# Sliding-window attention in pairs of tiles, with 64-column score pieces and one shared block of small triangles

## The chip, the cores and the metric

The kernel runs on one core of a Trainium2 chip. A core has TensorE (matmuls, here PE; its weight loads are PEld), VectorE (DVE), ScalarE (ACT), GpSimd (POOL) and SyncE (SP), which only issues transfers. Each engine works off its own list of instructions in order; semaphores tie the lists together. The metric is the device time of one execution in microseconds (us), lower is better.

## What is computed

One transformer block on x of 2048 rows and 448 columns, in bf16. The conditioning vector gives six rows (shift, scale and gate of each half). With h a layer norm of x, scaled and shifted:

```
q, k, v = h @ wqkv                      # 16 heads of 28
scores  = q k^T / sqrt(28), kept where 0 <= i - j < 256, else -1e9
x = x + ga * (softmax(scores) @ v) @ wo
h = layernorm(x) * (1 + cb) + sb
z = gelu(h @ w_in)                      # 1792 columns: z1 and z2, 896 each
g = w_sp @ layernorm(z2) + b_sp         # w_sp is 2048 x 2048
x = x + gb * (z1 * g) @ w_out
```

## The kernel before

The rows are 16 tiles of 128. All work is cut into operations, each with a name, an engine (or a choice of engines), what it needs and which buffers it holds. A stored list, `ORDER`, gives the order of all operations: a number is an operation by its order of creation, `/n` picks its buffer and `.n` its engine. `Planner.emit` (L115) turns this into one list for each engine, with waits. So nothing is planned at run time: each engine goes through its list and stops where a wait isn't met.

**Projections.** `project` (L775 on) multiplies the transposed, modulated rows hT by the weights. The 448 rows of contraction lie in four chunks of 128, of which chunks 1 and 2 overlap; one half of one of them holds zeros or is left out. A chain of four full matmuls gives one group of four heads of Q or K for a block of rows (blocks of 1, 1, 2, 4, 4 and 4 tiles), or V of one tile. ScalarE or VectorE evicts the result into QKT or Vaug (L806, L809, L818, L821). In the second half of the block, z2 (`z2m`) and z1 (`z1m`) come from hT and w_in in the same chunks; there the class `Pair` (L734) makes two chains of three full matmuls and one operation `_r` with both half chunks, 64 rows each, which run beside each other in two row strips of the array.

**Attention** (L862 to L960), tile by tile. For tile j the keys of tiles j-2, j and j-1 matter. For each of these a visit of 16 matmuls (`s_mm`, 28 rows by 128 columns, heads in four row strips of the array) puts scores of all 16 heads into four banks. Two exponentials (L908, 128 x 1024 elements each, two banks) write them to a slot of PT. For the tiles j-2 and j the window cuts a triangle, and GpSimd zeroes it with an affine select over 512 32-bit pairs (L914). Eight matmuls (`pv_fn`, columns of 32 beside each other) multiply each slot by V, with the sum of the exponentials in a column of ones. So a whole tile has three visits, six exponentials and four selects; in all there are 90 exponentials and 60 selects.

VectorE transposes the result (`oq`, L940), takes the reciprocal, VectorE or GpSimd normalises (`nrm`, L945), VectorE transposes again (`oT`, L949), four matmuls multiply by wo, and VectorE adds to x (`x1`, L959). Layer norm, a transposing transfer and a modulation give the second hT.

**The second half.** GELU on ScalarE (L1018, L1014 for z2, L1037 for z1), the layer norm of z2 on VectorE, then 28 products of 16 full matmuls each with the transposed w_sp (`G`), whose parts lie where QKT, Vaug and PT lay, so that their transfers wait for the end of attention. VectorE adds and multiplies (L1106, L1108); `out` matmuls, a last addition (L1128) and the stores end the kernel.

**Shapes on TensorE.** Score visits run in four row strips, products with V in four column strips, half chunks in two row strips, the rest on the whole array. `column_tiles` (L104) lets whole matmuls that stand next to products with V run as four column strips. All matmuls go through `mm` (L451 to L457), so they share these lines in the profile and are told apart by tiles and shapes.

## Time and profile before

| | us |
|---|---|
| time, median of 3 runs | 269.65 (269.1 to 269.99) |
| span of the profiled execution, first to last instruction | 267.2 |
| between the span and the median | 2.45 |
| DVE / ACT / POOL busy in the span | 166.0 / 133.2 / 103.8 |

The profile gives no separate time for its own execution; its span stands beside the runs' median. Its rows name an engine, a line, an operation and the tiles, with the count; then busy time in total, the mean of one in ns, and the engine's idle time just before with what ended it. Sums by stage give, for a stretch of the span, the busy time and the count of each engine. The chain is followed back from the last instruction through what released each step.

### The profile page before, as it was taken

The page shows a single profiled execution, that of the slowest core. Times are in us where ns is not written, and L with a number is a line of the kernel's source. Part 1 is how long each engine was busy: PE and PEld are TensorE (multiplying, and loading weights), DVE is VectorE, ACT ScalarE, POOL GpSimd, SP SyncE. Part 2 cuts the span into 40 slices and gives each one's busy share as a digit, 9 for nine tenths or more (in the row PEclk, how much of TensorE's full clock was granted, in tenths as well). Part 3 has the DMA queues.
Part 4 walks back from the last instruction along what each step waited for, and adds up shares of the span by engine and source line. Part 5 has one row for each costly group of instructions (what it writes and reads, how often), then busy time and mean ns, then how long its engine had stood idle before and what let it go on. Part 6 is the DMA issues. An engine that isn't in the chain of part 4 may idle for free.

```text
span 267.2 us, 7093 instructions
## 1 busy us (share of the span) xinstructions
PE 258.8 (97%) x3059; PEld 127.8 (48%) x3059; DVE 166.0 (62%) x389; ACT 133.2 (50%) x182; POOL 103.8 (39%) x163
## 2 busy tenths in 40 slices
PE   6799999999999899999999999999999999999996
PEld 2676455554554444544444444444444444444553
DVE  4789987878789999488888730722033071327553
ACT  4899899999999999977687100000000000000100
POOL 3774799997989866436532300000000000000000
PEclk9999999999999999999999999999999999999999
DMA  6974260371998341789799950000000000000133
GB/s 225 352 194 56 42 178 5 71 122 23 172 212 195 65 100 39 124 118 164 157 191 215 165 97 0 2 0 0 0 0 2 0 0 0 2 0 17 52 101 108
DMA packets 61020, 23.83 MB, mean 89 GB/s; under 512 B 49854, under 2 KB 60861, under 8 KB 60989
## 3 DMA queue, kind: packets, MB, share of 16 engines
q1 hardware_dynamic: 60715, 22.92, 41.0%
q8 instruction: 24, 0.39, 0.7%
q10 hardware_dynamic: 274, 0.46, 0.5%
q14 instruction: 7, 0.06, 0.1%
HBM read 9.47 MB, written 1.84 MB: 42 GB/s over the span
## 4 chain that ended last, share of the span: by engine, by line
PE 76%; ACT 14%; DMA 3%; DVE 3%; SPq 1%; POOL 1%; issue 1%
PE ps L457 71%; ACT PT L908 12%; PE ps L454 5%; DMA wqk_raw<-in_A_wqkv_dram 2%; DMA hT<-xn 2%; ACT QKT L806 1%; DVE w_out_sb L964 1%; POOL PT L914 1%; ACT hT L683 1%; SPq L488 1%; DVE oq L940 1%; DVE oT L949 0%; PE ps L772 0%; POOL xn L620 0%; SPq L505 0%
## 5 line engine op out<-in xcount | busy, mean ns | idle before, releaser
L908 ACT ACTIVATE PT<-ps 128x1024 bf16<-128x1024 f32 x90 | 84.5, 1059 | 2.3 <-PE ps L457 1.7
L1037 ACT ACTIVATE z1T<-ps 128x512 bf16<-128x512 f32 x28 | 15.1, 599 | 100.9 <-PE ps L457 100.8
L1106 DVE TENSOR_TENSOR tmpg<-ps,bsp_bc 128x512 bf16<-128x512 f32 x28 | 18.8, 688 | 60.9 <-PE ps L457 60.6
L457 PE MATMUL ps<-QKT,z 128*128 128x512 bf16 x224 | 50.0, 379 | 0.0
L914 POOL TENSOR_SCALAR_AFFINE_SELECT PT<-PT 128x512 f32<-128x512 f32 x60 | 36.8, 635 | 5.1 <-ACT PT L908 5.1
L457 PEld LDWEIGHTS ps<-QKT,z 128*128 128x128 bf16 x224 | 21.9, 98 | 26.4 <-ACT z2raw L1018 0.2
L607 POOL TENSOR_TENSOR rs_all<-ve_all,neghalf 128x1 f32<-128x1 f32 (+2 forms) x27 | 18.6, 692 | 27.8 <-DVE ve_all L606 26.7
L457 PE MATMUL ps<-w_spC,z 128*128 128x512 bf16 x112 | 25.8, 379 | 0.0
L457 PE MATMUL ps<-w_spD,z 128*128 128x512 bf16 x112 | 25.8, 379 | 0.0
L457 PE MATMUL ps<-hT,w_in_sb 128*128 128x512 bf16 (+1 forms) x101 | 25.2, 380 | 0.0
L457 PE MATMUL ps<-w_in_sb,hT 128*128 128x448 bf16 (+1 forms) x110 | 24.4, 353 | 0.4 <-DVE oq L940 0.2
L620 POOL TENSOR_SCALAR xn<-x_sb,rs_all,nm_all 128x512 bf16<-128x512 bf16 x26 | 20.2, 782 | 4.7 <-DVE nm_all L611 3.0
L457 PE MATMUL ps<-w_out_sb,z1T 128*128 128x448 bf16 (+2 forms) x119 | 21.9, 341 | 0.0
L457 PE MATMUL ps<-hT,WQK 128*128 128x512 bf16 (+2 forms) x123 | 21.1, 307 | 0.7 <-ACT QKT L806 0.7
L599 DVE BATCH_NORM_STATS2 st_all<-x_sb 128x6 f32<-128x448 bf16 x32 | 19.3, 615 | 3.0 <-DMA x_sb<-in_A_x_dram 2.8
L599 DVE BATCH_NORM_STATS2 st_all<-z2raw 128x6 f32<-128x448 bf16 x32 | 19.3, 618 | 2.1 <-ACT z2raw L1018 1.8
L457 PE MATMUL ps<-QKT 28*128 28x128 bf16 x720 | 18.3, 217 | 1.5 <-ACT PT L908 1.4
L457 PEld LDWEIGHTS ps<-QKT 28*128 28x128 bf16 x720 | 10.4, 92 | 15.6 <-ACT PT L908 11.3
L809 DVE CAST QKT<-ps 128x512 bf16<-128x512 f32 (+2 forms) x26 | 16.1, 624 | 2.8 <-PE ps L457 1.8
L457 PEld LDWEIGHTS ps<-w_spC,z 128*128 128x128 bf16 x112 | 10.9, 98 | 13.4 <-DVE ve_all L606 0.4
L457 PEld LDWEIGHTS ps<-w_spD,z 128*128 128x128 bf16 x112 | 11.0, 98 | 13.2
L457 PEld LDWEIGHTS ps<-w_out_sb,z1T 128*128 128x128 bf16 x119 | 11.6, 98 | 9.9
(93 smaller groups left out, 319.3 us busy)
## 6 DMA issues: line engine op xcount, KB each, us to landing
wmod_sb<-in_w_mod_dram SPq DMA_DIRECT2D x8, 224.0 KB, 4.3
w_in_sb<-in_B_w_in_dram SPq DMA_DIRECT2D x8, 224.0 KB, 4.3
out_dram<-fin SPq DMA_DIRECT2D x16, 112.0 KB, 1.7
x_sb<-in_A_x_dram SPq DMA_DIRECT2D x3, 448.0 KB, 6.6
bsp_bc<-in_B_b_sp_dram SPq DMA_DIRECT2D x1, 512.0 KB, 4.7
wqk_raw<-in_A_wqkv_dram SPq DMA_DIRECT2D x1, 452.0 KB, 5.6
wmod_sb<-in_w_mod_dram SPq DMA_DIRECT2D x1, 448.0 KB, 4.5
wmod_sb<-in_w_mod_dram ACTq DMA_DIRECT2D x1, 448.0 KB, 4.8
```

What stands on the lines that cost most here:

```text
L454: last = e.matmul(out_[32 * j:32 * j + 32], lhsT=lhsT[:, 32 * j:32 * j + 32], rhs=rhs, start=st, stop=sp, tile_position=(0, 32 * j), **kw)
L457: return e.matmul(out_, lhsT=lhsT, rhs=rhs, start=st, stop=sp, **kw)
L488: return load(name, prio, lambda e: e.dma_start(x_sb[:, t0:t0 + n, :], x_d[:, t0:t0 + n, :]), n * 128 * D * 2, order=order)
L599: st = [dve("%sst%d" % (name, i), prio, dve_ns(D), lambda e, i=i, s_=s_: e.bn_stats(st_all[:, slot, t, i, :], s_()), deps, tens) for i, s_ ...
L607: r = pool(name + "rs", prio, 420 + 148 * n, lambda e: e.tensor_tensor(rs_all[:, slot, t0:t1], ve_all[:, slot, t0:t1], neghalf[:, t0:t1], ...
L620: return e.tensor_scalar(dst, src, rs_all[:, slot, t:t + 1], nm_all[:, slot, t:t + 1], ALU.mult, ALU.add)
L683: last = e.activation(d, s_, ACT.Identity, bias=a, scale=k)
L809: return e.tensor_copy(QKT[:, g, cols], ps[:, ten.slot, 0:w])
L908: e_op = P.op("E%d_%d" % (j, ui), pr, [("act", 925, lambda e, e_in=e_in, e_out=e_out: e.activation(e_out(), e_in(), ACT.Exp, scale=SCALE)) ...
L914: ready = pool("M%d_%d" % (j, ui), pr - 50, pool_ns(512), lambda e, pt=pt, pat=pat, cm=cm, cmp=cmp: e.affine_select(out=pt32(pt.slot), in_ ...
L1037: g = P.op("z1g%d_%d" % (tb, ft), pr - 19, [("act", act_ns(512), lambda e: e.activation(z1T[:, ft, tb * 512:(tb + 1) * 512], ps[:, ten.slo ...
L1106: a = dve("ga%d_%d" % (tb, ft), pr, dve_ns(512), lambda e, tb=tb, ten=ten, tg=tg: e.tensor_tensor(tmpg[:, tg.slot, :], ps[:, ten.slot, :], ...
```

## The change

Tiles 0 and 1 stay as they were. From tile 2 on attention goes by pairs (j, j+1) in five visits, each with two exponentials:

- E, twice (two groups of heads each): keys of tiles j-2 and j-1, that is 64 columns of the first and 192 of the second for each head, eight 64-column pieces to a bank.
- C, once: the four small triangles of 64 by 64 for each head and tile (keys of the own tile's half, and of the tile two back), 64 matmuls of 28 rows by 64 columns and 64 moving columns, in four row strips and two column strips. Two selects split the block: `Mb` writes one kind of triangle to a buffer of its own, then `Ma` zeroes the other kind in place.
- L, twice: keys of tiles j and j+1, again 192 and 64 columns.

E and L each need one select over 256 pairs. In all there are 76 exponentials and 88 selects. A product with V (`PV..._p`, `_m`, `_d` for the tiles two back, one back and own) now takes its two 64-column halves from different slots, and needs both E or L visits of its heads. The slots lie in PT, and six more in rows of z2 and z1T that are free until attention ends; the z2 normalisations of tiles 5 to 8 and the GELUs of z1's last columns wait for all products with V.

`Pair` is replaced by `chunks`: one chain of three full matmuls and one half one, `_r`, free to stand anywhere. The projections of the blocks from the third on use it too, and there the order picks for each `_r` whether it runs whole or half. The warm-up matmuls go from 22 to 14. `ORDER` is a new list of 1735 operations. Among other things it gives ScalarE 2 more evictions of Q or K, 4 of V and 5 of z2, GpSimd 5 normalisations and 7 xn fewer and 5 modulations more, and in the first microseconds takes five operations off ScalarE's list ahead of its first exponential. Its numbers are left out here.

```diff
+    PTS = [z2_off + 9 * FH * 2 - 6144 + 2048 * i for i in range(3)] + [z1_end - 6144 + 2048 * i for i in range(3)] + [pt_off + 2048 * i for i in range(NPT)]
+    assert 6144 <= 4 * FH * 2 and z1_off + 8 * 6 * D <= z1_end - 6144
+
+    def ptv(slot, off, dims):
+        v = arena[:, PTS[slot] // 2 + off:PTS[slot] // 2 + off + 1]
+        return bass.AP(v.tensor, v.offset, [list(v.ap[0])] + dims)
+
+    def pt32(slot, off, dims):
+        v = arena[:, PTS[slot] // 2 + 2 * off:PTS[slot] // 2 + 2 * off + 2].bitcast(F32)
+        return bass.AP(v.tensor, v.offset, [list(v.ap[0])] + dims)
...
+    def chunks(name, prio, side, opts, deps, stat, mov, n, joint=None, idx=0, rprio=None, padded=False):
+
+        ten = joint if joint else Ten(opts, guard=True)
+        acc = Acc()
+
+        def out_ap():
+            return ps[:, joint.got[idx][1] if joint else ten.slot, 0:n]
+        ops = []
+        for c_ in (0, 3, 1 + side):
+            o = [None]
+
+            def fn(e, c_=c_, o=o):
+                return mm(e, out_ap(), stat(c_, slice(0, 128)), mov(c_, slice(0, 128)), acc.first is o[0], acc.last is o[0])
+            o[0] = pe("%s_%d" % (name, c_), prio, mm_ns(n), fn, deps(c_), [ten], order=ops[:1], accs=[acc])
+            ops.append(o[0])
+        c_, rows, pos = (2, slice(64, 128), (64, 0)) if side == 0 else (1, slice(0, 64), (0, 0))
+        r = [None]
+
+        def rest(e):
+            return mm(e, out_ap(), stat(c_, rows), mov(c_, rows), acc.first is r[0], acc.last is r[0], tile_position=pos)
+
+        def whole(e):
+            return mm(e, out_ap(), stat(c_, slice(0, 128)), mov(c_, slice(0, 128)), acc.first is r[0], acc.last is r[0])
+        r[0] = P.op(name + "_r", prio if rprio is None else rprio, [("pe", mm_ns(n), f) for f in ([whole] if padded else []) + [rest]],
+                    [deps(c_), padded or []], [ten], order=ops[:1], mode=(FREE, 64) if padded else 64, accs=[acc])
+        ops.append(r[0])
+        return ops, ten
...
+                elif b >= 2:
+                    ops, ten = chunks("qk%d_%d" % (b, g), p_, g // 4, B_D, lambda c_, u=u, g=g: [t_wqkp[u // 2][3][(g // 4, c_)], hT_op[b][c_]],
+                                      lambda c_, r, g=g: WQK[r, c_, 4 * g:4 * g + 4, :].rearrange("p a b -> p (a b)"), lambda c_, r: hT[r, c_, cols], w, padded=[z_wq[g // 4]])
+                    proj[b].extend(ops)
...
+    def exp_op(name, pr, s_op, tens, e_in, e_out, pt):
+        return P.op(name, pr, [("act", 925, lambda e: e.activation(e_out(), e_in(), ACT.Exp, scale=SCALE))], [s_op, t_exp0], tens + [pt], table="exp")
+
+    def keep(name, pr, n, slot_in, slot_out, off, dims, pattern, base, cm, cmp, deps, tens):
+        return pool(name, pr, pool_ns(n), lambda e: e.affine_select(
+            out=pt32(slot_out.slot, off, dims), in_=pt32(slot_in.slot, off, dims), pattern=pattern, compare_op=cmp, fill=0.0, base=base, channel_multiplier=cm), deps, tens)
+
+    def pv_op(name, pr, gp, kb, acc, pv_ten, tens, deps, mov):
+        o = [None]
+
+        def fn(e):
+            last = None
+            for s_ in range(2):
+                for g in range(4):
+                    last = mm(e, pvo(pv_ten.slot, g, 2 * gp + s_), Vaug[:, kb, 4 * g + 2 * gp + s_, :], mov(g, s_),
+                              s_ == 0 and acc.first is o[0], s_ == 1 and acc.last is o[0], tile_position=(0, 32 * g), skip_group_check=True)
+            return last
+        o[0] = pe(name, pr + G["pv"], 8 * 14, fn, [deps, V_op[kb]], tens + [pv_ten], accs=[acc], mode=33)
+        return o[0]
...
+    def tile_pair(j):
+        unit = {}
+
+        def visit(kind, gh, pr):
+            gs = (2 * gh, 2 * gh + 1) if kind != "C" else (0, 1, 2, 3)
+            tens = [Ten(B_S), Ten(B_S)]
+            k0 = {"E": j - 2, "L": j, "C": j}[kind]
+
+            def s_mm(e):
                 last = None
+                if kind == "C":
+                    for g in gs:
+                        for t in (j, j + 1):
+                            for h, kt in ((0, t), (1, t - 2)):
+                                for r in range(4):
+                                    c = 128 * g + 64 * (t - j)
+                                    last = mm(e, ps[64 * h:64 * h + 64, tens[r // 2].slot + r % 2, c:c + 64],
+                                              QKT[32 * r:32 * r + DH, 4 + g, kt * 128 + 64 * h:kt * 128 + 64 * h + 64],
+                                              QKT[32 * r:32 * r + DH, g, t * 128 + 64 * h:t * 128 + 64 * h + 64], True, True, tile_position=(32 * r, 64 * h))
+                    return last
+                for gl, g in enumerate(gs):
+                    for kt, q0, n, c in ((k0, j * 128, 1, 6), (k0 + 1, j * 128, 3, 0)) if kind == "E" else ((k0, j * 128 + 64, 3, 2), (k0 + 1, j * 128 + 192, 1, 0)):
+                        for r in range(4):
+                            v = ps[:, tens[r // 2].slot + r % 2, 64 * (c + gl):64 * (c + gl) + 1]
+                            last = mm(e, bass.AP(v.tensor, v.offset, [list(v.ap[0]), [128, n], [1, 64]]), QKT[32 * r:32 * r + DH, 4 + g, kt * 128:(kt + 1) * 128],
+                                      QKT[32 * r:32 * r + DH, g, q0:q0 + 64 * n], True, True, tile_position=(32 * r, 0))
+                return last
+            keys = {"E": (j - 2, j - 1), "L": (j, j + 1), "C": (j - 2, j - 1, j, j + 1)}[kind]
+            deps = [QK_op[(g, blk[j])] for g in gs] + [QK_op[(4 + g, blk[k])] for g in gs for k in keys]
+            nm = "%s%d_%d" % (kind, j, gh)
+            s_op = pe("S" + nm, pr - 50, 270, s_mm, deps, tens, mode=32)
+            pair_S.setdefault(j, []).append(s_op)
+            for gp in range(2):
+                pt = Ten(B_C if kind == "C" else B_EL)
+                nmu = "%s%d" % (nm, gp)
+                ready = exp_op("E" + nmu, pr, s_op, [tens[gp]], lambda ten=tens[gp]: ps[:, ten.slot:ten.slot + 2, :].rearrange("p b n -> p n b"),
+                               lambda pt=pt: ptv(pt.slot, 0, [[2, 512], [1, 2]]), pt)
+                if kind == "E":
+                    ready = keep("M" + nmu, pr, 256, pt, pt, 256, [[64, 4], [1, 64]], [[0, 4], [-1, 64]], 0, 1, ALU.is_gt, [ready], [pt])
+                elif kind == "L":
+                    ready = keep("M" + nmu, pr, 256, pt, pt, 0, [[64, 4], [1, 64]], [[0, 4], [1, 64]], 64, -1, ALU.is_ge, [ready], [pt])
                 else:
+                    ptb = Ten(B_B)
+                    dims = [[64, 8], [1, 64]]
+                    mb = keep("Mb" + nmu, pr, 512, pt, ptb, 0, dims, [[0, 8], [-1, 64]], -64, 1, ALU.is_gt, [ready], [pt, ptb])
+                    ma = keep("Ma" + nmu, pr, 512, pt, pt, 0, dims, [[0, 8], [1, 64]], 0, -1, ALU.is_ge, [ready, mb], [pt])
+                    unit[("B", gp)] = (ptb, mb)
+                    ready = ma
+                unit[(kind, gh, gp)] = (pt, ready)
+        for n_, (kind, gh) in enumerate((("E", 0), ("E", 1), ("C", 0), ("L", 0), ("L", 1))):
+            visit(kind, gh, j + 0.4 * n_)
+
+        def seg2(a, oa, b, ob):
+            return ptv(a.slot, oa, [[(PTS[b.slot] - PTS[a.slot]) // 2 + ob - oa, 2], [2, 64]])
+        for t in (j, j + 1):
+            odd = t - j
+            pv_ten, acc = Ten(B_PV), Acc()
+            pvs = []
+            for gp in range(2):
+                E, L = [unit[("E", gh, gp)] for gh in range(2)], [unit[("L", gh, gp)] for gh in range(2)]
+                C, B = unit[("C", 0, gp)], unit[("B", gp)]
+                A = L if odd else E
+                pvs.append(pv_op("PV%d_p%d" % (t, gp), t, gp, t - 2, acc, pv_ten, [E[0][0], E[1][0], B[0]], [E[0][1], E[1][1], B[1]],
+                                 lambda g, s_, E=E, B=B, odd=odd: seg2(E[g // 2][0], 128 * (6 - 2 * odd + g % 2) + s_, B[0], 256 * g + 128 * odd + s_)))
+                pvs.append(pv_op("PV%d_m%d" % (t, gp), t, gp, t - 1, acc, pv_ten, [A[0][0], A[1][0]], [A[0][1], A[1][1]],
+                                 lambda g, s_, A=A, odd=odd: ptv(A[g // 2][0].slot, 128 * (4 * odd + g % 2) + s_, [[256, 2], [2, 64]])))
+                pvs.append(pv_op("PV%d_d%d" % (t, gp), t, gp, t, acc, pv_ten, [C[0], L[0][0], L[1][0]], [C[1], L[0][1], L[1][1]],
+                                 lambda g, s_, C=C, L=L, odd=odd: seg2(C[0], 256 * g + 128 * odd + s_, L[g // 2][0], 128 * (2 - 2 * odd + g % 2) + s_)))
+            pv_of[t] = (pvs, pv_ten)
...
-            need = [rs] + (proj_all if t >= 9 else raw_users)
+            need = [rs] + (proj_all if t >= 9 else raw_users) + (all_PV if 5 <= t <= 8 else [])
...
-                    z1T[:, ft, tb * 512:(tb + 1) * 512], ps[:, ten.slot, :], ACT.Gelu_apprx_tanh))], deps + mod_done, [ten], table="gelu")
+                    z1T[:, ft, tb * 512:(tb + 1) * 512], ps[:, ten.slot, :], ACT.Gelu_apprx_tanh))], deps + mod_done + (all_PV if ft >= 5 else []), [ten], table="gelu")
...
-    for i in range(22):
+    for i in range(14):
```

310 lines of the change are left out of this document (135 added, 175 removed).

## The prediction

> **What bounds the kernel now.** I began with the page's first part and its chain, which name TensorE, and then asked how far to trust them: the sums by stage, the instructions in order of time, and the waits.
>
> ```profile
> span 267.2 us, 7093 instructions
> PE 258.8 (97%) x3059; PEld 127.8 (48%) x3059; DVE 166.0 (62%) x389; ACT 133.2 (50%) x182; POOL 103.8 (39%) x163
> ...
> PE 76%; ACT 14%; DMA 3%; DVE 3%; SPq 1%; POOL 1%; issue 1%
> ```
>
> TensorE is called busy for 97% of the span and carries 76% of the chain; ScalarE comes second with 14%. The sums by stage (PE, PEld, DVE, ACT, POOL from left to right) show where ScalarE's part lies:
>
> ```profile
> 0.00:10.00 10.00, 7.22 (x79) 3.87 (x82) 4.75 (x18) 5.71 (x12) 4.18 (x17) 1.00 0.83 263
> 10.00:20.00 10.00, 9.26 (x178) 6.69 (x164) 8.82 (x28) 9.63 (x27) 7.96 (x12) 1.00 0.88 252
> 20.00:30.00 10.00, 9.83 (x271) 5.82 (x270) 9.04 (x23) 9.16 (x15) 5.22 (x9) 1.00 0.28 40
> 30.00:70.00 40.00, 39.95 (x865) 20.88 (x867) 32.75 (x72) 39.10 (x44) 37.44 (x54) 1.00 0.41 92
> 70.00:120.00 50.00, 47.92 (x981) 24.03 (x972) 42.12 (x98) 47.11 (x55) 34.53 (x51) 1.00 0.67 121
> 120.00:264.60 144.60, 144.60 (x711) 66.50 (x709) 68.12 (x153) 22.46 (x34) 14.47 (x25) 1.00 0.29 57
> ...
> 75.00:92.00 17.00, 15.35 (x403) 8.25 (x392) 15.19 (x36) 17.00 (x20) 14.94 (x22) 1.00 0.82 168
> ```
>
> From 120 to 264.6 us TensorE has no gap at all and ScalarE is nearly idle. From 30 to 70 us ScalarE is busy for 39.10 of 40 us, but TensorE, given other work in the same order, for 39.95. Only between 75 and 92 us does a full ScalarE (17.00 of 17.00) leave TensorE 1.65 us short. So the exponentials are not the length of this kernel: they cost what TensorE loses waiting for them.
>
> A matmul's busy time runs past the start of the next, so "busy" can hide waiting. The starts in order of time tell more:
>
> ```profile
> 41.62 1.27 PE L457 MATMUL ps<-hT,WQK 128*128 128x512 bf16 x5
> 42.82 0.40 PE L457 MATMUL ps<-QKT 28*128 28x128 bf16 x16
> 43.16 1.69 PE L457 MATMUL ps<-hT,WQK 128*128 128x512 bf16 x7
> 44.77 0.40 PE L457 MATMUL ps<-QKT 28*128 28x128 bf16 x16
> 45.11 1.05 PE L454 MATMUL ps<-hT,WQK 128*32 128x512 bf16 x16
> 45.98 0.87 PE L457 MATMUL ps<-PT,Vaug 128*32 128x128 bf16 x48
> 46.78 0.40 PE L457 MATMUL ps<-QKT 28*128 28x128 bf16 x16
> ...
> 161.69 1.46 PE L457 MATMUL ps<-QKT,z 128*128 128x512 bf16 x6
> 162.98 1.03 PE L457 MATMUL ps<-w_spC,z 128*128 128x512 bf16 x4
> 163.84 2.32 PE L457 MATMUL ps<-QKT,z 128*128 128x512 bf16 x10
> ```
>
> In the late stage six 512-column matmuls take 162.98 - 161.69 = 1.29 us, 0.215 us each: 0.42 ns a column. A visit of 16 score matmuls, four beside each other in four row strips, streams 4 x 128 columns, 0.215 us, but 43.16 - 42.82 = 0.34 us pass until the next work starts. The seven full matmuls behind it need 7 x 0.215 = 1.51 us and take 1.61. So each change of TensorE's tile shape costs about 0.12 us (0.10 and 0.125). Sorting the old order by tile shape I count 119 changes, 115 of them from the first score visit on: some 14 us, the largest loss there is. What is truly waited for is small:
>
> ```profile
> PE ps L457 <- ACT PT L908: 1.4, 4, 0.4
> PE ps L457 <- DVE oq L940: 0.2, 1, 0.2
> PE ps L454 <- DVE hT L697: 0.2, 1, 0.2
> ...
> PEld ps L457 <- ACT PT L908: 11.7, 30, 0.6
> ...
> 83.51 0.40 PE L457 MATMUL ps<-QKT 28*128 28x128 bf16 x16 [0.43 <-ACT PT L908]
> ```
>
> (Both answers cover 20 to 120 us; the last row, in order of time, is the longest of the four waits.) The weight loads' 11.7 us are mostly the shape change and the running matmul; the stages above leave 0.17 + 0.05 + 2.08 = 2.3 us of open gap from 20 to 120 us. With what hides under running matmuls I call the recoverable waiting 2.3 to 5 us. The Trainium skill, in "Trainium Kernel Development and Optimization" under "Performance Expectations", says that matmul busy time is a bad measure because matmuls are pipelined; by it the 97% would hide more, and the starts above agree that busy is not the same as streaming.
>
> **The change, part by part.**
>
> Exponentials, 90 to 76, and what the new order moves onto ScalarE and off GpSimd:
>
> ```profile
> L908 ACT ACTIVATE PT<-ps 128x1024 bf16<-128x1024 f32 x90 | 84.5, 1059 | 2.3 <-PE ps L457 1.7
> L818 ACT ACTIVATE Vaug<-ps 128x448 bf16<-128x448 f32 x3 | 1.6, 545 | 0.0
> L914 POOL TENSOR_SCALAR_AFFINE_SELECT PT<-PT 128x512 f32<-128x512 f32 x60 | 36.8, 635 | 5.1 <-ACT PT L908 5.1
> L531 POOL TENSOR_SCALAR_AFFINE_SELECT ident<-ident 128x128 bf16<-128x128 bf16 x1 | 0.3, 292 | 0.1
> L945 POOL TENSOR_TENSOR o_sb<-oq,rec_all 128x448 bf16<-128x448 f32 x13 | 12.2, 942 | 8.5 <-DVE rec_all L941 8.4
> L620 POOL TENSOR_SCALAR xn<-x_sb,rs_all,nm_all 128x512 bf16<-128x512 bf16 x26 | 20.2, 782 | 4.7 <-DVE nm_all L611 3.0 <-DVE nm_all L637 1.7
> ```
>
> 14 x 84.5/90 = 13.1 us leave ScalarE; it takes over eleven evictions (2 of Q or K, 4 of V, 5 of z2, near 0.545 us each: 6 us) and gives two early ones to other engines: about 8 us lighter. GpSimd's selects go from 60 to 88, of which 56 have 256 columns. No row shows that form; it lies between the 128-column select (0.292) and the 512-column one (0.635), and on the line between them near 0.41: 56 x 0.41 + 32 x 0.635 = 43.3 us against 38.1, +5.2 (-0.4 to +17.8 with 0.31 to 0.635 each). GpSimd loses five normalisations (0.942), seven xn (0.782) and gains five modulations: it ends some 2 us lighter. Both engines get slack; neither decides. Of the waiting of 2.3 to 5 us I take **-2.0 us** (from +1 to -4.5, since the new order has waits of its own: each diagonal product now needs one shared block and two late blocks, so three exponentials and their selects, and all that stands behind it in TensorE's order waits too). Two waits are new beyond attention: the GELUs of z1's columns from 640 on and the z2 normalisations of tiles 5 to 8 now wait for every product with V, because their rows hold exponentials until then. Behind the first such GELU stand ScalarE's other GELUs, and TensorE's banks behind those; in the new order it comes after the last products are issued, so I cost it at nothing, with up to 1 us if the last product is late (inside the +1 above).
>
> Score matmuls. Before, a tile has three visits; now a pair has five. E and L visits keep 16 matmuls and 512 columns' worth of streaming, 0.215 us (in each row strip 64 then 192 columns, 0.225 with a little for the short ones). The shared visit issues 64 matmuls of 64 columns on strips of 28 rows by 64 columns, a form that no row shows. If all eight strips stream together it is 8 x 64 columns, 0.22 us. At the other end stand the shortest matmuls of the trace, on the whole array, one behind the other:
>
> ```profile
> 6.36 0.44 PE L457 MATMUL ps<-sc_sb,wmod_sb 128*128 128x1 bf16 x12
> 6.67 0.60 PE L457 MATMUL ps<-warm 128*128 128x256 bf16 x4
> ```
>
> 12 in 0.31 us: 0.026 us each, so 64 in a row would be 1.65 us. The nearer row is the score visit: its sixteen matmuls start in four groups and the next weights are loaded meanwhile. I take twice the best, 0.43 us. Streaming of all score visits: before 46 visits, 45 x 0.215 = 9.7 us; now 3 x 0.215 for the first two tiles (two half visits and two whole), 28 x 0.225 and 7 x 0.43: 10.0 us, **+0.3** (-1.2 to +8.9).
>
> "TensorE: Matmul & The Clock Gate" of the Trainium skill, under "Back-to-back issue gap", puts a matmul of up to 64 columns at about 60 cycles, near 25 ns; the 0.026 us above agrees for the whole array. "TensorEngine Tiling (Array Packing)", under "Restrictions", adds that column tiling switches the fast weight load off, which speaks against this visit. Read as a cost of each of the 64 instructions, the first gives an estimate of 1.6 us a visit; read as one of each strip, the 0.43 stands.
>
> Half matmuls. Of 46 projection chains that always ended in a full fourth matmul, 27 may now end in a half one (19 stay whole), and a half one saves only when another half runs beside it on the other 64 rows. I matched them in the new order, segment by segment: 8 in a group with a partner; 9 stand alone and save nothing, and the early z2 halves, two of which now share a side, give a little back. In columns, 1.15 us less: **-1.15** (0 if halves do not overlap).
>
> Shape changes. In the new order I count 142, but 16 before the first score visit (4 before) and 126 from there on (115): fewer score visits, more half-matmul groups. 11 x 0.12 = **+1.3 us** (+1.0 to +1.7).
>
> The head. ScalarE's first exponential waits behind its own queue:
>
> ```profile
> 13.17 1.03 ACT L908 ACTIVATE PT<-ps 128x1024 bf16<-128x1024 f32 x1
> ...
> L806 ACT ACTIVATE QKT<-ps 128x128 bf16<-128x128 f32 x15 | 3.2, 282 | 0.3 <-PE ps L772 0.3
> L722 ACT ACTIVATE WQK<-wqk_raw 128x512 bf16<-128x512 bf16 x2 | 1.3, 626 | 2.3 <-DMA wqk_raw<-in_A_wqkv_dram 2.3
> ```
>
> Five operations leave that queue ahead of it: one spread of weights (0.626), one hT eviction and three QKT evictions (0.282), some 1.9 us; they go to VectorE and GpSimd, or later. The weights still land when they do (2.3 us of that idle time), and TensorE has twelve more shape changes there, 1.4 us, covered as long as it waits for those weights anyway (2.78 us idle in the first 10 us). On SP's queue two early loads change places (x of tiles 2 and 3 behind the last small weight rows) and one piece of wo goes ahead of the V weights; what the first exponential needs keeps its place. Eight warm-up matmuls less change nothing while it waits. I take **-0.5** (-1.5 to +1.4). The tail, matmuls without a gap, keeps its work; products with w_spC and w_spD still wait for the end of attention.
>
> Sum: -2.0 + 0.3 - 1.15 + 1.3 - 0.5 = -2.05, and I keep **-1.7** for the extra rounds and loads of the short matmuls that the columns don't count (0.35). The span goes from 267.2 to 265.5. No time of the profiled execution itself is listed; the runs are 269.1 to 269.99, median 269.65, that is 2.45 us around this span. So 265.5 + 2.45 = **268.0 us**, 0.6% less. What a measurement of this kernel can tell from no change is about 0.3%, 0.8 us.
>
> **The rivals.**
> - Full TensorE, no change. Every relieved wait is filled by shape changes and the shared visit: waiting -1, head 0 leave -2.05 + 1.0 + 0.5 + 0.35 = -0.2, so 269.4. For it: 39.95 of 40 us busy beside a ScalarE that is as full. Against it: the 1.65 us of 75 to 92 us are open gaps under a full ScalarE.
> - The shared visit goes one by one, slower. Its place is seven visits at the even tiles, its price 7 x (1.65 - 0.43) = +8.5 us: 268.0 + 8.5 = 276.5. My forecast turns to slower when a visit passes 0.43 + (1.7 + 0.8)/7 = 0.79 us. For it: 64 weight loads of a kind not shown, half of each strip's time. Against it: the sixteen score matmuls of today hide theirs.
> - A longer way from score to product. Exponential, first select, second select (0.94 + 2 x 0.635 = 2.2 us) stand in a row before the diagonal product, against 1.57 today. If TensorE stops 0.63 us at each of seven pairs, that is +4.4: 272.4. Against it: the order puts those products one or two visits later.
> - Better than I say: all 5 us of waiting go and the shared visit streams at its best: -3.0 - 1.5 more, 263.5.
>
> **How the numbers follow.** Forecast (with the better case) 0.55, no change 0.17, one-by-one visit 0.16, longer way 0.12. So faster by over 0.3% 0.55, within 0.17, slower 0.28. The range takes in the better case nearly whole, no change and the longer way, and leaves the one-by-one visit mostly out: 263.8 to 274.0. The likeliest case alone: 266 to 269.
>
> **What would show it.** Right: ScalarE's total near 125 us; PEclk 1.00; a shared visit of 64 matmuls whose next work starts 0.5 to 0.6 us after its first; TensorE's waits for ScalarE between 75 and 92 us gone; the gapless stage starting about 2 us earlier. Wrong: shared visits of over 0.8 us; waits of TensorE or its weight loads for GpSimd's selects; gaps before 120 us that VectorE ends; or a first exponential later than 13.2 us.

## The result and the profile after

The changed kernel takes 273.11, 273.16 and 275.02 us, 273.8 in the mean, against 269.69 us before (median of four): ratio 1.0153, interval 1.0118 to 1.0188, so 1.5% slower. A fourth execution, of 278.31 us at a granted clock of 0.994, is left out of this, as disturbed executions are left out of every ratio below. I had forecast 268.0 us and faster: the sign is wrong, and the times lie around the upper end of my range (274.0). The profiled execution took 273.11 us with a span of 271.2, 4.0 us more than the span before.

The page first, then the sums by stage (PE, PEld, DVE, ACT, POOL, granted clock):

```profile
span 271.2 us, 7838 instructions
...
PE 260.1 (96%) x3428; PEld 127.9 (47%) x3428; DVE 167.0 (62%) x387; ACT 123.2 (45%) x175; POOL 105.2 (39%) x184
...
PE 75%; POOL 9%; DVE 7%; ACT 4%; DMA 2%; issue 1%; DVEq 0%; POOLq 0%
```

```profile
20.00:30.00 10.00, 8.52 (x242) 4.73 (x242) 9.72 (x22) 8.03 (x12) 5.79 (x9) 1.00 0.45 112
30.00:70.00 40.00, 39.15 (x1019) 20.24 (x1018) 34.10 (x76) 34.35 (x40) 29.60 (x51) 1.00 0.55 123
70.00:120.00 50.00, 47.33 (x1187) 24.64 (x1189) 40.39 (x92) 43.89 (x55) 42.40 (x72) 1.00 0.54 94
120.00:264.60 144.60, 144.60 (x730) 65.80 (x723) 65.03 (x148) 22.65 (x35) 16.63 (x28) 1.00 0.26 53
75.00:92.00 17.00, 16.07 (x483) 9.03 (x484) 13.31 (x29) 14.52 (x18) 15.12 (x26) 1.00 0.58 94
```

ScalarE did get its slack: 34.35 of 40 us from 30 to 70 us, where it had 39.10, and 14.52 of 17 from 75 to 92 us, where it had all 17. The chain now names ScalarE with 4% in place of 14%, and GpSimd with 9% in place of 1%. GpSimd is hardly busier in total (105.2 us, before 103.8), but its work has moved to a later stage: from 30 to 70 us it works 29.60 us in place of 37.44, from 70 to 120 us 42.40 in place of 34.53. All of the loss is there when attention ends: the last product with V starts 4.0 us later (112.6 us before, 116.6 now; the times behind min/median/max are the first and the last start):

```profile
L457 PE MATMUL ps<-PT,Vaug x720: 217/220/233, 22.1 to 112.6; 128*32 128x128 bf16 x180
...
L468 PE MATMUL ps<-arena,Vaug x720: 217/220/236, 23.1 to 116.6; 128*32 128x128 bf16 x180
```

The waits of TensorE from 20 to 120 us show the exchange (us in total, times, longest):

```profile
PE ps L468 <- POOL arena L885: 1.7, 4, 0.9
PE ps L468 <- issue: 1.0, 1, 1.0
PE ps L468 <- ACT arena L882: 0.9, 3, 0.4
PE ps L465 <- DVE hT L708: 0.4, 1, 0.4
PE ps L465 <- DVE x_sb L1054: 0.3, 1, 0.3
```

Four waits for GpSimd's selects (L885) are new, as is one stop with no semaphore behind it, 1.0 us. In order of time, a V projection that waits for VectorE, the first shared visit with its stop, a product with V that waits, a later shared visit without a stop, and the longest wait of a product:

```profile
27.16 0.56 PE L465 MATMUL ps<-wv_sb,hT 128*32 128x448 bf16 x8 [0.35 <-DVE hT L708]
...
28.39 0.68 PE L468 MATMUL ps<-QKT 28*64 28x64 bf16 x61
30.05 0.22 PE L468 MATMUL ps<-QKT 28*64 28x64 bf16 x3 [0.98 <-issue]
...
36.29 0.30 PE L468 MATMUL ps<-arena,Vaug 128*32 128x128 bf16 x8 [0.37 <-POOL arena L885]
...
42.84 0.71 PE L468 MATMUL ps<-QKT 28*64 28x64 bf16 x64
43.48 0.39 PE L468 MATMUL ps<-hT,WQK 128*128 128x512 bf16 x1
...
75.19 0.53 PE L468 MATMUL ps<-arena,Vaug 128*32 128x128 bf16 x24 [0.90 <-POOL arena L885]
```

What this last product waits for stands in GpSimd's own list: it waits 1.34 us for an exponential and then works through nine selects in a row, until 75.04 us.

```profile
70.82 4.22 POOL L885 TENSOR_SCALAR_AFFINE_SELECT arena<-arena 128x256 f32<-128x256 f32 x9 [1.34 <-ACT arena L882]
75.03 1.52 POOL L631 TENSOR_SCALAR xn<-x_sb,rs_all,nm_all 128x512 bf16<-128x512 bf16 x2
```

From the starts of all matmuls I took off what streams and 0.095 us for each shape change; what is left is standing still. By this estimate it is 10.3 us before and 13.8 after, some 3.4 more of the span's 4.0; streaming and shape changes together are the other 0.6. Stops of 0.1 us and more, by the work whose end comes last before them:

| TensorE stands for | before | after |
|---|---|---|
| GpSimd's selects, ahead of products with V | 0 | 3.0 |
| the stop inside the first shared visit | 0 | 1.2 |
| ScalarE's exponentials | 2.0 | 1.3 |
| VectorE's and GpSimd's other work | 1.8 | 2.4 |

So the question for the runs: is it the selects' longer way and the shared visit (theory L), is it only where the order puts things (theory A), or was there little to gain from ScalarE to begin with?

### The profile page after: what moved, and what is told of

Same layout as the page of the kernel before. It is cut to its first block, busy times and chain, and to the rows that moved or that the text cites. A ratio compares the mean times of both kernels' runs of the same rounds, so it can differ in the third digit from the quotient of the medians.

```text
span 271.2 us, 7838 instructions
## 1 busy us (share of the span) xinstructions
PE 260.1 (96%) x3428; PEld 127.9 (47%) x3428; DVE 167.0 (62%) x387; ACT 123.2 (45%) x175; POOL 105.2 (39%) x184
## 4 chain that ended last, share of the span: by engine, by line
PE 75%; POOL 9%; DVE 7%; ACT 4%; DMA 2%; issue 1%; DVEq 0%; POOLq 0%
PE ps L468 67%; PE ps L465 8%; POOL arena L885 6%; ACT arena L882 3%; DMA hT<-xn 2%; POOL hT L708 1%; DVE hT L708 1%; DVE x_sb L1054 1%; DVE st_all L610 1%; DVE xn L632 1%; POOL rs_all L618 1%; ACT QKT L816 1%; POOL xn L631 1%; DVE QKT L819 1%; DVE hT L699 1%
## 5 line engine op out<-in xcount | busy, mean ns | idle before, releaser
L882 ACT ACTIVATE arena<-ps 128x1024 bf16<-128x1024 f32 x76 | 72.5, 1035 | 8.1 <-PE ps L468 7.8
L468 PE MATMUL ps<-QKT,z 128*128 128x512 bf16 x224 | 52.1, 379 | 0.0
L885 POOL TENSOR_SCALAR_AFFINE_SELECT arena<-arena 128x256 f32<-128x256 f32 (+1 forms) x88 | 43.6, 526 | 9.8 <-ACT arena L882 6.0
L468 PE MATMUL ps<-hT,WQK 128*128 128x512 bf16 (+4 forms) x143 | 25.3, 305 | 0.5 <-DVE mv_all L613 0.5
L468 PE MATMUL ps<-w_in_sb,hT 128*128 128x448 bf16 (+1 forms) x89 | 22.5, 354 | 0.0
L708 POOL TENSOR_SCALAR hT<-hT,modT 128x512 bf16<-128x512 bf16 (+1 forms) x24 | 17.0, 716 | 10.8 <-DMA hT<-xn 10.8
L468 PE MATMUL ps<-arena,Vaug 128*32 128x128 bf16 x720 | 18.4, 221 | 2.0 <-POOL arena L885 1.7
L468 PE MATMUL ps<-QKT 28*64 28x64 bf16 (+3 forms) x944 | 17.8, 210 | 2.0 <-issue 1.0
L468 PEld LDWEIGHTS ps<-QKT 28*128 28x128 bf16 (+1 forms) x944 | 11.3, 98 | 13.5 <-ACT arena L882 8.2
L468 PEld LDWEIGHTS ps<-arena,Vaug 128*32 128x32 bf16 x720 | 12.8, 95 | 10.0 <-POOL arena L885 2.2
```

What stands on the lines that cost most here:

```text
L468: return e.matmul(out_, lhsT=lhsT, rhs=rhs, start=st, stop=sp, **kw)
L708: return e.tensor_scalar(hT[:, c_, cols], hT[:, c_, cols], modT[:, base_col + 4 + c_:base_col + 5 + c_], modT[:, base_col + c_:base_col + ...
L882: return P.op(name, pr, [("act", 925, lambda e: e.activation(e_out(), e_in(), ACT.Exp, scale=SCALE))], [s_op, t_exp0], tens + [pt], table= ...
L885: return pool(name, pr, pool_ns(n), lambda e: e.affine_select(out=pt32(slot_out.slot, off, dims), in_=pt32(slot_in.slot, off, dims), patte ...
```

## The experiments

Every ratio is against the kernel before, run beside it on the same chip; the changed kernel's own is 1.0153. A time is the median of all executions, with their range; gains and losses are taken from the ratios.

**What the relief of ScalarE is worth** (the kernel before, `exp` in the place of the activation):

```diff
+    def short(v, slot):
+        if len(v.shape) != 3 or slot not in filled:
+            return v
+        return v[:, 0:256, :]
...
+        r = e.activation(short(out, slot) if cut else out, short(in_, slot) if cut else in_, ACT.Exp, scale=SCALE)
...
```

> Left out: in the kernel before, half the columns of the exponentials for keys of the tile one back (about 28 of 90), so that ScalarE loses some 12 us, about the 13.1 us that the change takes off it, and nothing else changes. The forecast put 2.0 us of TensorE's waiting on that relief: 267.7 if it was sized rightly. If waits for ScalarE are mostly replaced by the next wait, 269 to 269.8.

269.40 us (268.87 to 269.91), ratio 0.9982, interval 0.9966 to 0.9998. Its exponentials:

```profile
L871 ACT ACTIVATE PT<-ps 128x1024 bf16<-128x1024 f32 x64 | 61.5, 1026 | 7.1 <-PE ps L457 6.7
...
L871 ACT ACTIVATE PT<-ps 128x512 bf16<-128x512 f32 x26 | 14.8, 608 | 2.0 <-PE ps L457 1.5
```

76.3 us in place of 84.5: 8.2 us less, not 12, and the time falls by 0.5 us (0.1 to 0.9 by the interval). In proportion, the 12.0 us by which the exponentials fell with the change (84.5 to 72.5) would give 0.7, at most 1.3. TensorE's waits from 20 to 120 us show why: those for exponentials halve (0.7 us, before 1.4), and others take their place, 1.9 us in all where it was 1.8:

```profile
PE ps L457 <- ACT PT L871: 0.7, 2, 0.4
PE ps L457 <- DVE oq L952: 0.5, 2, 0.3
PE ps L457 <- DVE w_out_sb L976: 0.4, 1, 0.4
PE ps L454 <- DVE wo_sb L855: 0.3, 1, 0.3
```

A larger cut in the changed kernel, half the columns of 62 of its 76 exponentials:

> Left out: in the changed kernel half the columns of every exponential from tile 2 on but the first in each slot (about 55), some 25 us of ScalarE. If ScalarE no longer decides (theory A and B both say that GpSimd's selects and VectorE do, with 1.3 us of TensorE's stops left to exponentials), 272.5 to 273.5, though each select starts 0.4 us sooner; if the exponentials are still the first link of every stop at a product, 271 or less.

272.08, 274.63, 277.48 and 281.73 us, ratio 1.0131, interval 1.0069 to 1.0193: no gain beyond the intervals, though the exponentials fall from 72.5 to 48.1 us. A gain of up to 2.5 us lies within the intervals, so that ScalarE no longer decides is likely and not shown.

**What the selects cost.** In the changed kernel, and as a control before:

```diff
     def keep(name, pr, n, slot_in, slot_out, off, dims, pattern, base, cm, cmp, deps, tens):
+        if slot_in is slot_out:
+            dims, pattern = [[dims[0][0], 1], dims[1]], [[pattern[0][0], 1], pattern[1]]
...
```

> The changed kernel with each in-place select cut to one 64-column piece (128 columns in the first two tiles); the second select of the shared block keeps its size. The mask is then only partly applied; all other work stays. Longer way from score to product: the seven stops of TensorE at products behind a select, 3.0 us in the profile of the changed kernel, mostly go, 270 to 271.5 us. Shape changes or the order as such: GpSimd is not what ends the stops that count, 273 to 275 us as before.

> The kernel before with each select cut from four groups of 128 columns to one; the mask is then only partly applied. Longer way: before, no product waited for a select (no stop over 0.1 us), so 269 to 270 us, no change. If cheaper selects help here as much as in the changed kernel, GpSimd is simply a general load and the shared block is not special: below 268 us.

272.33 us, ratio 1.0092 (1.0057 to 1.0127), so 0.6% or 1.6 us less than the changed kernel (0.3 to 3.0 by the two intervals); the control 269.84, 0.9978 (0.9957 to 0.9999), with a median equal to that of the kernel before beside it. GpSimd loses about as much in both (105.2 to 88.3 us busy, before 103.8 to 83.6). So before, cutting the selects returns about 0.2% or nothing; in the changed kernel it returns, by the middle of a wide interval, over a third of the loss, and its four waits for selects are gone from the profile. With only the early and late selects cut:

```diff
+        if n == 256:
+            dims, pattern = [[dims[0][0], 1], dims[1]], [[pattern[0][0], 1], pattern[1]]
```

> Left out: three of four pieces of the 56 selects over 256 pairs (early and late visits), while the shared block's two selects stay whole. The profile of the changed kernel names a late block's select at six of eight stops. If GpSimd's queue of those selects is what the products wait for: most of what cutting all gave, 272.3 to 272.8. If the two selects in a row of the shared block are (the rival as I put it): 273.5 to 274.5.

270.79, 271.76, 275.01 and 275.34 us, ratio 1.0144 (1.0076 to 1.0212): too wide to tell the late selects from the shared block's pair. And the other way round, selects that nobody waits for, added to the kernel before:

```diff
+    z_more = pool("zmore", -90, 300, lambda e: e.memset(more[:, :], 1.0))
+    for i in range(28):
+        z_more = pool("more%d" % i, 0, pool_ns(256), lambda e: e.affine_select(
...
```

> The kernel before with 28 more selects on GpSimd (192 pairs each, on a buffer of their own that nothing else reads, one behind each select of tiles 9 to 15), some 10 us of GpSimd work that no other engine waits for, where GpSimd was busy 34.5 of 50 us. By theory C: five or more of VectorE's operations are stretched, and the time rises by 1 to 4 us. If GpSimd's slack takes them up, as the forecast had it: within 0.5 us of the kernel before.

272.12 us (271.34 to 272.44), 1.0082 (1.0053 to 1.0110): 2.2 us by the ratio, 2.5 by the medians, for 28 selects with no consumer (10.4 us of GpSimd's time), in a stretch where GpSimd had 15 us to spare. The stage from 70 to 120 us, and TensorE's waits in it, which before were 1.4 us for exponentials and 0.2 for `oq`:

```profile
70.00:120.00 50.00, 44.96 (x967) 22.66 (x965) 41.56 (x92) 46.53 (x54) 42.80 (x76) 1.00 0.75 118
```

```profile
PE ps L459 <- ACT PT L910: 1.1, 3, 0.6
PE ps L459 <- DVE rec_all L943: 1.0, 1, 1.0
PE ps L459 <- DVE oq L942: 0.9, 2, 0.6
PE ps L459 <- POOL PT L916: 0.6, 2, 0.4
PE ps L459 <- DVE w_out_sb L966: 0.4, 1, 0.4
```

GpSimd is at 42.80 us, where the changed kernel has it (42.40), and TensorE waits for selects and, more, for VectorE. An engine with 30% idle isn't free here: the added selects make the results behind them late, in GpSimd's own list and, as the last section tells, in some of VectorE's operations. Which of the two costs more was not separated.

**What the shared visit costs.** Only 16 of its 64 matmuls are left, in all seven visits (the edit below) and in the first alone:

```diff
-                        for t in (j, j + 1):
-                            for h, kt in ((0, t), (1, t - 2)):
+                        for t in (j,):
+                            for h, kt in ((0, t),):
```

> The changed kernel with 16 instead of 64 matmuls in each shared visit: three quarters of its scores are not computed. Shared visit as the cause: 7 x 0.4 us of streaming, and the 1.2 us gap inside the first one, 4 us less, 269 us. Longer way: products still wait for the same selects, TensorE only arrives earlier, 1 to 2 us less, 271 to 272 us; the gap of 1.2 us is seen to go, stay or move in the profile.

> Left out: 48 of the 64 matmuls of the first shared visit alone (the one behind which TensorE stops 1.2 us with no semaphore); the six others are whole. If that stop comes from 128 instructions of TensorE in half a microsecond at that place, it goes and the time falls by 1.0 to 1.5 us, to 272.6 to 273.1, nearly all that thinning all seven visits gave. If the stop is paid back elsewhere, or belongs to the place and not to the instructions, 274.

All seven: 272.40 us, 1.0071 (1.0034 to 1.0109), some 2.2 us less for 336 fewer matmuls, which stream 8.3 ns each, 2.8 us. A whole visit streams 0.53 us where I had 0.43 (the next work starts 0.64 us after its first matmul, 42.84 to 43.48 above, with the shape change). The first alone: the stop inside it is gone in its profile,

```profile
28.04 0.32 PE L468 MATMUL ps<-QKT 28*64 28x64 bf16 x16
28.29 2.35 PE L468 MATMUL ps<-hT,WQK 128*128 128x512 bf16 x10
```

but the time is 277.53 us (274.55 to 278.64), 1.0263, outside both expectations. So the stop comes with the many instructions at that place, and taking it away gained nothing at the end; why the time rose is open.

The traces say more of such stops. Queue q8 loads instructions, in 24 packets before and 27 now, for 6118 and 6856 matmuls and weight loads:

```profile
q8 instruction: 24, 0.39, 0.7%
...
q8 instruction: 27, 0.44, 0.7%
```

One of these loads runs from 27.62 to 28.50 us, and TensorE goes on 1.55 us behind its end. In the profiles of all runs 20 stops without a semaphore are longer than 0.26 us, 19 of them in the changed kernel and its variants, and every one ends 1.2 to 1.6 us behind such a load. So TensorE probably stood for instructions that had not come; no run moves the loads. The versions with all seven visits thinned have 24 packets and no such stop, and part of what thinning returns may be that. Selects and visits cut together:

> Left out: in the changed kernel three quarters of every in-place select's pieces (7/8 for the shared block's) and 48 of the 64 matmuls of each shared visit, both cuts together. Alone they gave 272.33 and 272.4 beside 274.1, so -1.8 and -1.7. If they are separate costs the two add: 270.6, the time of the kernel before plus 0.8. If both only shift the same waits, 272 to 272.5.

270.04 us, 0.9955 (0.9918 to 0.9993): 2.0% or 5.3 us under the changed kernel, where the two alone gave 1.6 and 2.2. So they are separate costs; that the sum is more than additive lies within the intervals. (It also leaves out work that the kernel before does, so it isn't a gain to be had.)

**Half matmuls and shape changes.** Ten lone half matmuls run whole (124 shape changes for 142), then all 27 (118); in the order the option `.1`, half, is dropped:

```diff
-316.1 ... 457.1 ...
+316 ... 457 ...
```

> The changed kernel with ten half matmuls that have no partner run whole: 124 shape changes of TensorE where there were 142, the columns streamed the same. Shape changes as the cause: 18 x 0.095 = 1.7 us less, 271.3 to 272.5 us. Longer way: TensorE comes to the same waits earlier and loses there what it gains, less than 0.8 us, 273 us or more.

> The changed kernel with all 27 half matmuls of its Q, K and V projections run whole, same computation and order: 118 shape changes in place of 142, and up to 1.15 us more columns. By the forecast's own terms: +1.15 - 24 x 0.12 = -1.7 beside the changed kernel, 272.4. If halves pay for themselves (or the time saved only turns into waits), 273.5 to 275.

273.97 us, 1.0128 (1.0090 to 1.0167), and 280.37 us (276.51 to 281.97), 1.0288 (1.0223 to 1.0352). The first is within the spread of the changed kernel; the second is slower, outside both expectations. So shape changes priced at 0.12 us each could not be bought back this way. That the time saved ahead of the products is waited out there is one reading: in the profile of the second, TensorE's waits from 20 to 120 us are 1.7 us for exponentials (0.9 in the changed kernel), 1.7 without a semaphore (1.0) and 1.4 for selects (1.7). It was not shown.

**Is it the order?** Five waiting products moved two to four groups later by hand, alone and with the 27 whole ones; for tile 9's (740):

```diff
-740/0 741 739 436 743 738 742
+741/0 739 436 743 738 742 740
```

> The changed kernel with five products with V moved later in the order by two to four matmul groups each (the diagonal ones of tiles 4, 9 and both of 12, and one of tile 2), where TensorE stood 2.7 us for GpSimd's selects. If the stops belong to the order of those few products: about 2 us less, 271.5 to 272.5. If the wait only passes to the next work (the selects end when they end): 273.5 to 274.5.

> Both of the two edits above together. If the effects add as the forecast's terms say: -1.7 - 2.0, 270.4, level with the kernel before. If both only shift waits, 273 to 274.

277.86 us (274.70 to 278.09), 1.0259 (1.0201 to 1.0316), slower than expected either way; with the whole ones too, 275.84, 280.29, 282.47 and 284.01 us, too far apart for a ratio, so that it tells nothing. Part of the wait passes on: in the first profile TensorE still stands for selects (1.2 us, three times), and 1.6 us, five times, without a semaphore. Then whole re-orderings from measured durations, each with a control:

> The changed kernel with the same 1735 operations, slots and engines in another stored order: single operations were shifted, by at most 40 places at a time, with the durations that the changed kernel's own trace gives, so that work which waits comes later and selects that are waited for come earlier. Theory A (the design is sound, its order has no slack where the new selects and evictions end late): the waiting of 13.8 us falls by 3 to 4 us, 269 to 271. Theory B (the longer way from score to product is paid whatever the order): 273 to 275.

> The same search for the kernel before, with its own durations, as a control: what a re-ordering by measured durations is worth where nothing new was added. By theory A its order already fits its durations: within 1 us of the kernel before (269 to 271). If it gains 2 us or more, then what the first of these runs gains is owed to searching and not to the change.

> The changed kernel, re-ordered by its own measured durations from 30 us to the end of attention only; everything before 30 us, every operation that waits for a load, and the gapless stage keep their places (the first re-ordering moved work in front of loads that had not landed, and TensorE stood still for 4 us at 20 us). Theory A (its order lacks slack where new selects and evictions end late): 270.5 to 272.5. Theory B (paid whatever the order): 273.5 to 275.

> The control: the kernel before, re-ordered in the same stretch by the same search and its own durations. Theory A: within 0.8 us of the kernel before (269.0 to 270.6), since its order fits. If it gains as much as the changed kernel does, re-ordering is worth that anywhere.

> The changed kernel re-ordered from 24 us to the end of attention so that, by its own measured durations, VectorE's modulations, normalisations and xn do not start while GpSimd works (5.4 us of stretched VectorE work before, under 1 us wanted). Theory C (VectorE and GpSimd block each other, and that sets much of the changed kernel's loss): stretched work under 2 us and a time of 270 to 272. If the stretched work goes and the time stays at 273.5 to 275, theory C is wrong; if the stretched work stays, nothing is told.

| re-ordered | kernel | median us (range) | ratio (interval) |
|---|---|---|---|
| from 20 us on | changed | 284.34 (281.77 to 285.96) | 1.0524 (1.0451 to 1.0596) |
| from 20 us on | before | 282.15 (280.58 to 282.57) | 1.0441 (1.0401 to 1.0480) |
| 30 us to the end of attention | changed | 274.62 (274.03 to 277.47) | 1.0199 (1.0143 to 1.0254) |
| 30 us to the end of attention | before | 273.30 (272.85 to 274.91) | 1.0140 (1.0104 to 1.0175) |
| without VectorE under GpSimd | changed | 278.57 (278.04 to 278.67) | 1.0324 (1.0277 to 1.0370) |

None helps, and the controls lose as well: my model of the order missed by more than the effect, so these runs neither bear out theory A nor rule it out. The first pair failed by a plain mistake: work stood in front of loads that had not landed (TensorE still for 4.0 us at 20 us, in the control for 2.8). The last was to take away the meetings of VectorE and GpSimd that are told below; about 12 stretched operations and 3.4 us of the 15 and 5.4 were left, so it settles nothing about them. No run that computes the whole block beats the kernel before.

## Why the prediction was wrong

- **What bounds the kernel before:** right. TensorE almost without a gap, ScalarE second, 0.095 to 0.12 us a shape change.
- **Exponentials and ScalarE's load:** right in size. ScalarE 123.2 us (125 forecast), the exponentials 12.0 us less (13.1 forecast).
- **"Of the waiting of 2.3 to 5 us I take -2.0 us":** this is the step that failed, and with it "both engines get slack; neither decides". Two things were wrong in it. The relief was oversized: 8.2 us off ScalarE in the kernel before are worth 0.5 us, so 12.0 about 0.7. I had read TensorE's open waits as ScalarE's to give back; in that run they turned into the next wait. And the waits that the change adds were undersized. I priced GpSimd by its total. The selects came out near the estimate (+6.8 us, 36.8 to 43.6 on the two pages; +5.2 forecast, with 0.431 and 0.693 us each in place of 0.41 and 0.635); GpSimd as a whole got no slack, 1.4 us more in place of 2 less. But a total says nothing on lateness:

```profile
L885 POOL TENSOR_SCALAR_AFFINE_SELECT arena<-arena 128x256 f32<-128x256 f32 x56 | 23.1, 431 | 3.1 <-ACT arena L882 2.9
L885 POOL TENSOR_SCALAR_AFFINE_SELECT arena<-arena 128x512 f32<-128x512 f32 x32 | 22.0, 693 | 6.7 <-PE ps L468 3.6 <-ACT arena L882 3.0
```

  Cutting the selects returns 1.6 us, and 28 selects with no consumer cost the kernel before 2.2 to 2.5. By the estimate above, standing still went up by 3.4 us, where waiting and head together were to take 2.5 off: that is 5.9 us, against 5.7 between the forecast span (265.5) and the measured one (271.2). The other terms are off by 0.2 the other way.
- **Score streaming +0.3:** the mechanism right, a visit 0.53 in place of 0.43 us: about 0.7 more for seven, +1.0 in place of +0.3. The one-by-one visit (1.65 us) did not come. The stop of 1.2 us in the first visit was not foreseen.
- **Half matmuls -1.15, shape changes +1.3:** streaming and changes together came out as +0.6 with the visits, close to my sum of +0.45. No run shows the terms one by one; running halves whole, fewer changes and more columns, gained nothing.
- **Head -0.5:** right where it was meant. The first exponential starts at 12.63 us in place of 13.17; it was lost again by 30 us (from 20 to 30 us TensorE is busy for 8.52 us, before 9.83).
- **Signs:** the waits for ScalarE between 75 and 92 us did shrink (0.3 us in place of 1.4), but 0.9 us for a select stand there now. TensorE's last gap of over 0.05 us ends at 108.2 us in place of 116.8, where 2 us earlier was forecast; as the last product with V yet starts 4.0 us later, it was a poor sign. And two of my signs for "wrong" stand in the profile: waits for GpSimd's selects, and gaps that VectorE ends.
- **Rivals:** "a longer way from score to product" (272.4, chance 0.12) comes nearest. Its place is right, eight stops of 0.14 to 1.08 us before products, 3.0 us in all; my argument against it, that the order puts those products one or two visits later, did not hold for the selects queued behind each other (nine in a row ahead of the longest wait). It should have had the larger chance: the profile before showed GpSimd at 37.44 of 40 us from 30 to 70 us, on the way to every diagonal product, and I called it slack. In the new order GpSimd's work moved behind 70 us, and the longest wait came there (75.19). "Full TensorE, no change" was right in that relieved waits are filled, but by other waits.

What stays open: the cuts don't divide the 4.0 us of the span. The selects' cut returns 1.6; the visits' cut returns 2.2, but it also takes away three quarters of a streaming that the forecast had in its sum, and only about 0.7 us of streaming and the stop of 1.2 are beyond it. Whether another order would save the design was not shown, nor why small edits of the order cost 3 us or more. Executions of one variant of the changed kernel differ by up to 9.7 us, those of the kernel before by up to 3.0, so a difference of 3 us between variants run four times is not far from the spread.

## What to carry to other kernels

Price an engine's added work by the results that come later for it, not by its total against its idle share: 28 selects that nobody waited for cost 2.2 to 2.5 us on an engine that was 30% idle. Before counting on relief of a second engine, shorten its work alone and measure what moves; here 8.2 us were worth 0.5. And be careful with a kernel whose order was fitted to its durations: both re-orderings of the kernel before by my model made it slower (1.4 and 4.4%), so a changed design is judged together with its order. How much of the loss here is the order's was not shown.

## What was not expected of the hardware

**VectorE lasts longer under GpSimd.** Before, the modulations, xn and normalisations on VectorE have one duration; in the changed kernel the same forms have maxima up to 2.5 times as long (min/median/max ns; before, then after):

```profile
L697 DVE TENSOR_SCALAR hT<-hT,modT x13: 330/403/414, 25.9 to 118.5; 128x512 bf16<-128x512 bf16 x13
...
L621 DVE TENSOR_SCALAR xn<-x_sb,mv_all,rs_all x2: 414/414/415, 5.0 to 16.7; 128x512 bf16<-128x512 bf16 x2
...
L945 DVE TENSOR_TENSOR o_sb<-oq,rec_all x3: 615/620/626, 97.4 to 111.5; 128x448 bf16<-128x448 f32 x3
```

```profile
L708 DVE TENSOR_SCALAR hT<-hT,modT x8: 328/408/1021, 25.0 to 136.4; 128x512 bf16<-128x512 bf16 x7, 128x256 bf16<-128x256 bf16 x1
...
L632 DVE TENSOR_SCALAR xn<-x_sb,mv_all,rs_all x9: 332/411/1033, 4.6 to 53.4; 128x512 bf16<-128x512 bf16 x9
...
L1040 DVE TENSOR_TENSOR o_sb<-oq,rec_all x8: 622/696/1074, 36.5 to 92.8; 128x448 bf16<-128x448 f32 x8
```

Compared form by form, one VectorE operation is stretched before (0.2 us) and about 15 after (some 5.4 us), all of them started while a GpSimd instruction ran. The clearest go on about 0.25 us before its end: the modulation of 1021 ns starts at 26.09 us under a GpSimd normalisation of 25.99 to 26.96, and the 0.35 us wait at 27.16 above is for it. No statistics, transpose or eviction is stretched in these two profiles. "SBUF — State Buffer" of the Trainium skill, under "Who interferes with whom", says that the two engines share a pair of ports as an exclusive lock, taken by `tensor_scalar` in its fast modes and by `tensor_tensor` with both inputs in SBUF; the rows agree. The change gave VectorE 5 normalisations and 7 xn more, just such operations, and GpSimd 28 selects more to meet them. With the 28 added selects the kernel before has 5 stretched ones (1.7 us). How much of the loss they are was not shown; with the selects cut, most of the stretched time is still there.

In the changed kernel with shortened exponentials one normalisation waited for eight selects in a row (92.66 to 96.37 us on GpSimd):

```profile
92.74 4.11 DVE L1052 TENSOR_TENSOR o_sb<-oq,rec_all 128x448 bf16<-128x448 f32 x1
```

**The clock halves after a stop, and not only after a long one.** In the first re-ordering of the changed kernel, at the end of its stop of 4.0 us, the granted clock (third column from the end) falls to half and stays low for some 10 us:

```profile
20.00:24.00 4.00, 0.50 (x3) 0.28 (x3) 2.65 (x8) 0.00 (x0) 1.11 (x2) 0.89 0.09 12
24.00:30.00 6.00, 5.05 (x35) 2.08 (x33) 3.31 (x4) 1.92 (x4) 0.00 (x0) 0.50 0.65 167
30.00:34.00 4.00, 4.00 (x57) 1.77 (x55) 1.65 (x5) 2.81 (x4) 0.65 (x2) 0.58 0.04 12
34.00:38.00 4.00, 3.98 (x151) 2.14 (x150) 3.24 (x7) 3.03 (x5) 3.83 (x7) 1.00 0.02 6
```

"TensorE: Matmul & The Clock Gate" of the Trainium skill, under "What's actually happening", puts the limit at about 3.4 us of idling; the stop here was longer, and the stops of up to 1.2 us in the changed kernel left the clock at 1.00. But the run with all 27 halves whole differs from it: its clock reads 0.51 from 56.4 to 59.8 us, where the longest stop just before was 0.74 us and TensorE had been busy for 2.26 of 3.40 us:

```profile
53.00:56.40 3.40, 2.26 (x76) 1.53 (x63) 1.43 (x5) 2.04 (x3) 0.68 (x2) 1.00 0.62 98
56.40:59.80 3.40, 3.34 (x64) 1.80 (x68) 1.84 (x4) 3.12 (x5) 2.25 (x4) 0.51 0.74 127
```

One such piece at half clock makes a mean of 0.994 over the span, which several executions of the variants show; it can cost TensorE up to 1.7 us. What sets it off was not tested.
